# A long convolution and a spectral mix on one core: the last pair's loads move from GpSimd's queue to SyncE's, and two loops share their evictions anew

## The chip, the cores and the metric

The kernel runs on one core of a Trainium2 chip. The metric is device time in microseconds (us) of one execution, the median of three runs. PE is TensorE, DVE VectorE, ACT ScalarE, POOL GpSimd, SP SyncE. A DMA that POOL issues goes through a queue that the profile calls software_dynamic (q0); one that SP issues goes through hardware_dynamic (q1).

## The reference

x is 8 x 5696 x 128, h is 5696 x 128, all float32. First x is convolved with h along the sequence, each of the 128 channels by itself; then 64 Fourier modes of the result are mixed by complex 128 x 128 matrices and added to it, and a rectified product with a 128 x 128 matrix is added to that:

```python
def _attn_ref(x, h):
    L = 2 * S
    Yf = np.fft.rfft(x, n=L, axis=1) * np.fft.rfft(h, n=L, axis=0)[None, :, :]
    return np.fft.irfft(Yf, n=L, axis=1)[:, :S, :]

def _moe_ref(x, w_r, w_i, w_ch):
    X = np.fft.rfft(x, axis=1)
    Xr, Xi = np.real(X[:, :64]), np.imag(X[:, :64])
    Y = np.zeros_like(X)
    Y[:, :64] = (einsum(Xr, w_r) - einsum(Xi, w_i)) + 1j * (einsum(Xr, w_i) + einsum(Xi, w_r))
    u = x + np.fft.irfft(Y, n=S, axis=1)
    return u + np.maximum(u @ w_ch, 0.0)
```

## The kernel before, in words

The transforms are matrix products with constants, in float16. The sequence of 5696 is split as 89 x 64. The eight batches are worked in four pairs (`g_` from 0 to 3).

**First transform.** Per pair, 32 tiles (`a_tile`, `j` from 0 to 31) of four matmuls of 180 columns each turn the pair's x (tile Xin) into As; each tile goes to PSUM in two banks and one engine, DVE or ACT, casts it into SBUF (L313 and L317). With `eng` "both" each engine casts half of it. For pair 0 all 32 stand in a loop ahead of the passes, with six `filter_tick`s (the transform of h) between them; without an engine named, `evac` hands the tiles out in turn, ACT first. For the other pairs, tiles 0 to 5 stand in the last ticks of the pass before, and tiles 6 to 31 in a loop at the border of two passes: ACT the even ones, DVE the odd ones, tile 31 both.

**Passes.** A pass over a pair has 23 ticks (NT) of four frequencies, and three more to drain. In tick t PE makes the second transform (`second`, As by M), DVE multiplies by the filter (`products`, writes U), and for tick t - 2 PE multiplies U by Wc and ACT casts the result into one of 6 to 10 buffers Zs and Zt; SP then stores that buffer, 256 KB, to a scratch in DRAM (zscr). For tick t - 3 PE gathers the 64 modes with G. A buffer is cast into again only when its store has landed: in the last pair ten buffers serve the first ten stores, and from then on eight of them go round, so that store 18 takes the buffer of store 10, 21 that of 13.

**Loads of the last pass.** While pair 3 is worked, the last stage's inputs are loaded: W (the mode matrices, four parts of 1 MB), S4a, S4b and IBs (constants of the way back), and the first chunks of zscr, ZT0 to ZT3, each in two parts (1024 and 416 KB). `early` says in which tick which of them is issued. All of them stand on POOL, and `pace` makes POOL wait for the DVE product of that tick. ZT2 and ZT3 also wait for the first 15 stores of the pair to have landed (SLACK). `load_id`, a load of 32 KB, is issued by SP in tick 14 and waits (`ZY`) for the stores of buffers 8 and 9. Behind the pass come WI and ZT4, on POOL.

**Last stage.** PE makes the mode mix (XT by W), transposes it, and then works 16 chunks of zscr (`u_z`, `u_tile`; four a pair, five buffers ZT0 to ZT4) into u, and `o_tile` multiplies by WI; ACT makes R, DVE adds, SP stores 256 or 512 KB to the output. `load_zt(i + 5)` is issued on SP as soon as chunk i has been read.

**Order and waits.** The kernel writes every engine's instructions in the order of the program. A `Recorder` works out which of them must wait for which, by tokens: an instruction waits for the last writer of what it reads, and for the readers and the writer of what it overwrites. A wait stands on the engine that issues, so a DMA that waits holds up everything behind it on SP or POOL. Each DMA takes a semaphore of a ring, and waits until the one that had it before has landed (ring "t", "p", "q" and so on; "z" has 10 for the stores).

Of the kernel before, what the change touches and what calls it, by code (L numbers as in the profile page):

```python
# [4 lines left out]
P = 128  # L5
# [118 lines left out]
def bass_long_conv_fft__then__afno_spectral_mix_kernel(nc, x, h, moe_w_r, moe_w_i, moe_w_ch, out):  # L124
    B, S, D = x.shape
    M = moe_w_r.shape[0]
# [6 lines left out]
    NP = B // 2  # L133
    KT = 4
    NT = (NK + KT - 1) // KT
# [15 lines left out]
    c, s = np.cos(th), np.sin(th)  # L151
# [6 lines left out]
    s4 = np.stack([back[:, None, None] * np.cos(ang), -back[:, None, None] * np.sin(ang)], axis=0)  # L158
    RB, PB = 2 * NK - P, 32
    rows = s4.transpose(1, 0, 2, 3).reshape(2 * NK, S)  # L160
    SH = (J // 2 + 1) * NQ
# [11 lines left out]
    ib = modes.copy()  # L173
    ib[:, 0] *= 0.5
    ib = ib.T.reshape(P, NQ, J).transpose(0, 2, 1)
# [11 lines left out]
    def const(name, a):  # L187
        return nc.inline_tensor(np.ascontiguousarray(a.astype(np.float16)), name=name)
# [4 lines left out]
    c_s4 = const("cS4", s4t)  # L193
    c_ib = const("cIB", ib.reshape(P, -1)[:, 0:SH])
    c_sg = nc.inline_tensor(np.ascontiguousarray(sg.astype(np.float32)), name="cSG")
    c_g = const("cG", g)
    wd = nc.dram_tensor("wscr", [P, 2 * M * D], F16, kind="Internal")
# [8 lines left out]
    def at(name, cols, dt, off):  # L206
        return nc.alloc_sbuf_tensor_at(name, [P, cols], dt, offset=off)
# [23 lines left out]
    NZL = NZS[-1]  # L231
# [25 lines left out]
    NC = 5  # L257
    ZP = ZB * 2 * D
# [5 lines left out]
    zt = [[at(f"ZT{i}{'ab'[p_]}", ZP, F16, zt_off[i][p_]) for p_ in range(2)] for i in range(NC)]  # L264
    ib_sb = at("IBs", S, F16, a_m)
    s4_sb = [at("S4a", S, F16, a_m + 2 * S), at("S4b", S, F16, a_as)]
# [13 lines left out]
    w_sb = at("W", 2 * M * D, F16, a_x)  # L280
# [4 lines left out]
    def ap(t, row, p0, n, off, dims):  # L285
        return bass.AP(t, p0 * row + off, [[row, n]] + [list(d) for d in dims])
# [5 lines left out]
    def pv(bank, off, dims, p0=0, n=P):  # L292
        return bass.AP(ps, p0 * 4096 + bank * 512 + off, [[4096, n]] + [list(d) for d in dims])

    R = Recorder(nc)
    for name, n in (("c", 16), ("x", 26), ("z", 10), ("w", 16), ("t", 10), ("s", 8), ("o", 12), ("p", 16), ("q", 10)):
        R.ring(name, n)

    def bank(i):
        return ("bank", i)  # L300
# [18 lines left out]
    def dma(eng, dst, src, ring, reads=(), writes=(), after=()):  # L319
        R.add(eng, lambda h_: h_.dma_start(dst, src), reads, writes, ring=ring, after=after)  # L320

    def mm(o, l, r, st, sp, reads, writes):
        R.add("tensor", lambda h_: h_.matmul(o, l, r, start=st, stop=sp), reads, writes)  # L323
# [3 lines left out]
    def once(key, toks):  # L327
        if key in first:
            return []
        first[key] = 1  # L330
        return list(toks)
# [3 lines left out]
    def turns(name, items):  # L335
        i = ring2.get(name, 0)
        ring2[name] = i + 1
        return items[i % len(items)]
# [41 lines left out]
    WD = [p_[3] for p_ in wp]  # L380
# [25 lines left out]
    XIN = [("xin", i) for i in range(2 * XC)]  # L406
# [33 lines left out]
    for j in range(16):  # L440
        t = turns("h", [0, 2, 4])
# [5 lines left out]
        for i in range(4 if j < 15 else 26):  # L447
# [4 lines left out]
             eng="vector" if j in (3, 7) else "scalar")  # L452
        if j % 2:
            i = j // 2 % 2 * XC + j // 4
# [4 lines left out]
    AST = [("as", j) for j in range(33)]  # L459

    def a_tile(j, slots, eng=None):
        t = turns("s", slots) if len(slots) > 1 else slots[0]
        for i in range(4):
            d = 4 * j + i
            mm(pv(t + i // 2, (i % 2) * 2 * NK, [[1, 2 * NK]]),
               ap(x_sb, XW, 0, P, d, [[XS, 2 * J]]), f1_sb[:, :], True, True,
               XIN + XZ + [("f1",)], [bank(t + i // 2)])
        if eng == "both":
            for i, e in enumerate(("vector", "scalar")):
                evac(bass.AP(a_sb, 4 * j + 2 * i, [[AW, P], [D, 2 * NK], [1, 2]]), pv(t + i, 0, [[1, 2 * NK], [2 * NK, 2]]),  # L470
                     [bank(t + i)], [("as", j + i)], 1.0 / 64, eng=e, after=once(("hp", j), HP))
            return
        evac(bass.AP(a_sb, 4 * j, [[AW, P], [D, 2 * NK], [2, 2], [1, 2]]),
             pv(t, 0, [[1, 2 * NK], [512, 2], [2 * NK, 2]]),
             [bank(t), bank(t + 1)], [("as", j)], 1.0 / 64, eng=eng, after=once(("hp", j), HP))


    def xtok(n):
        return [("xt", n, p_) for p_ in range(2)]
# [30 lines left out]

    def load_w(i):
        w = 2 * M * D // 4
        dma("gpsimd", w_sb[:, i * w:(i + 1) * w], bass.AP(wd, i * w, [[2 * M * D, P], [1, w]]),
            "p", WD, [("w", i)] + (XIN if i == 0 else []), after=pace)

    H_ALL = [("h", t, 0) for t in range(NT)] + [("h", t, 1, p0) for t in range(NT) for p0 in (0, J)]
    U_ALL = [("u", i) for i in range(NU)] + [("xs", i) for i in range(NXS)] + \
# [1 line left out]
    M_ALL = [("m", i) for i in range(MP)]  # L519
# [3 lines left out]
    ZX = [("zs", i, b) for i in range(NZ, NZL) for b in range(2)]  # L523
    zt_old = [(H_ALL, H_ALL), (AST, AST), (AST, AST), (H_ALL, H_ALL), (M_ALL[3:6], G_ALL)]

    def load_zt(i, eng="sync", more=()):
        g_, c_ = divmod(i, J // ZB)
        for part, (p0, r0, n) in enumerate(((0, 0, P), (PB, P, RB))):
            old = list(once(("zt", i % NC, part), zt_old[i % NC][part])) + list(more) + pace
            dma(eng, bass.AP(zt[i % NC][part], p0 * ZP, [[ZP, n], [1, ZP]]),  # L530
                bass.AP(zs, (g_ * 2 * NK + r0) * J * 256 + c_ * ZB * 256, [[J * 256, n], [1, ZP]]),
                "q" if eng == "gpsimd" else "t", [("zd", g_, s_) for s_ in range(NT)], [("zt", i % NC, part)], after=old)

    def clear_zt(i):
        z32 = zt[i][1][0:PB, :].bitcast(U32)
        R.add("gpsimd", lambda e: e.memset(z32, 0), (), [("zt0", i)], after=list(zt_old[i][1]) + pace)

    def load_ib():
        dma("gpsimd", ib_sb[:, 0:SH], c_ib.ap(), "p", (), [("ib", 0)], after=M_ALL[0:2] + pace)

    def reflect(eng, t, n, col, key, after):
        MN = S - SH
# [6 lines left out]

    def load_s4(part):  # L550
        n = PB + RB if part else P
        dma("gpsimd", s4_sb[part][0:n, 0:SH], bass.AP(c_s4, part * SH, [[2 * SH, n], [1, SH]]), "p", (),
            [("s4", part, 0)], after=pace + (AST if part else M_ALL[1:4]))

    V, A = "vector", "scalar"
    border = {NT - 1: [(0, 0, V)], NT: [(1, 2, V), (2, 0, V)], NT + 1: [(3, 2, A), (4, 0, V)], NT + 2: [(5, 2, V)]}
    early = {3: lambda: load_w(2), 5: lambda: load_w(3), 8: lambda: load_s4(1),
             10: lambda: clear_zt(0),
             11: lambda: load_zt(0, "gpsimd"),
             14: lambda: (load_id(), clear_zt(1)),  # L560
             15: lambda: load_zt(1, "gpsimd"),
             16: lambda: load_s4(0),
             18: lambda: load_ib(),
             NT - 2: lambda: (load_zt(2, "gpsimd", SLACK), load_zt(3, "gpsimd"), clear_zt(2), clear_zt(3))}
    pace = []
    SLACK = [("zd", NP - 1, s_) for s_ in range(NT - NZL)]

    def load_id():
        dma("sync", id_sb[:, :], bass.AP(c_w, 2 * P, [[3 * P, P], [1, P]]), "c", (), [("id",)], after=ZY)
# [144 lines left out]
    for i in range(NXH):  # L714
        x_load(1, i, x_h[i], xtok(i), [t_ for r_ in XR for t_ in r_])
    FOUR = [0, 2, 4, 6]
    for j in range(32):
        a_tile(j, FOUR)
        if j >= 11 and j % 3 == 2 and (j - 11) // 3 < LH:
            h_ = turns("s", FOUR)  # L720
            filter_tick((j - 11) // 3, [h_, h_ + 1])
    keep(16, turns("s", FOUR))
    for g_ in range(NP):
        if g_ == NP - 1:
            load_w(0)
            load_w(1)
        for t in range(NT + LM):
            tick(g_, t)
            if g_ == 0 and t < 2:
                keep(8, 4)  # L730
            assert g_ + 1 < NP or not wp
            if g_ == NP - 1 and t in early:
                pace[:] = [("u", min(t, NT - 1) % NU)]
                early[t]()
        evac(bass.AP(xt, 2 * g_ * XTW + M, [[B * XTW, P], [XTW, 2], [1, P]]), pv(MB, 0, [[P, 2], [1, P]]),
             [bank(MB)], [("xt", g_)], 1.0 / 64, eng="scalar", after=[("ag", k) for k in range(NS + 2 * XN, NK)])
        evac(bass.AP(xt, 2 * g_ * XTW, [[B * XTW, P], [XTW, 2], [1, M]]), pv(MB, M, [[P, 2], [1, M]]),
             [bank(MB)], [("xtn", g_)], -1.0 / 64, eng="vector" if g_ + 1 == NP else "scalar", after=[("ag", k) for k in range(NS + 2 * XN, NK)])
        if g_ + 1 < NP:
            for j in range(6, 32):  # L740
                a_tile(j, [(4, 6, 0, 2)[(j - 7) % 4] if j > 6 else 0], "both" if j == 31 else V if j % 2 else A)
                if j == 31:
                    keep(8, 6)
                if wp and j % 2 == 1:
                    dst, src_, ring, tok = wp.pop(0)
                    dma("gpsimd", dst, src_, ring, (), [tok], after=[("as", j)])
# [2 lines left out]
    pace[:] = []  # L749
    load_wi()  # L750
    for i in range(4, NC):
        load_zt(i, "gpsimd")
        clear_zt(i)

    LSLOT = [0, 2, 4, 6]
# [62 lines left out]
    for hb in range(2):  # L818
        evac(bass.AP(y_sb, hb * 32 * B, [[2 * M * B, P], [B, 32], [M * B, 2], [1, B]]),
             pv(6 + hb, 0, [[2 * B, 32], [B, 2], [1, B]]), [bank(6 + hb)], [("y", hb)], eng="vector" if hb else "scalar",  # L820
             after=ZY)
# [66 lines left out]
    for g_ in range(NP):  # L888
        last = g_ == NP - 1
        order = [(c_, b) for b in range(2) for c_ in range(NCH)] if last else [(c_, b) for c_ in range(NCH) for b in range(2)]  # L890
        for n, (c_, b) in enumerate(order):
            i = NCH * g_ + c_
# [46 lines left out]
```

## Time and profile before

| what | us |
|---|---|
| median of three runs | 384.41 |
| lowest, highest | 383.37, 386.99 |
| profiled execution | 387.21 |
| its span, first to last instruction of the program | 385.1 |
| PE busy in the span | 362.4 (94%) |
| ACT busy | 314.3 (82%) |
| DVE busy | 296.6 (77%) |
| POOL busy | 85.2 (22%) |
| passes of pairs 0 to 3 begin (first second transform) | 43.5, 106.8, 162.2, 217.7 |
| last cast of the last pass ends | 262.6 |
| last instruction of the chain | 381 |

The table's times count from the first instruction of the program in the profiled execution. PE's busy time is a model of pipelined matmuls, so 94% is not 94% of what PE can do. A PE clock of 1.00 is the full one. DMA traffic is told per queue: packets, MB moved, and the time that its packets took as a share of 16 engines' time; shares of two queues that overlap can add up to more than 100%.

### The profile page before, as it was taken

To read this page: it belongs to the slowest core of one execution; us is meant where nothing else is said; L and a number is where in the kernel's file an instruction comes from. 1 tells how busy PE (TensorE), PEld (TensorE's weight loads), DVE (VectorE), ACT (ScalarE), POOL (GpSimd) and SP (SyncE) were. 2 spreads that over 40 slices of the span, in tenths; PEclk is the share of its full clock that TensorE was granted. 3 is DMA by queue.
4 is the path that set the end of the run, shared out by engine and by line. 5 is a ranking of instruction groups with operands and counts; after the bars stand their busy time and mean duration, and the time that the engine had idled before them with its cause. 6 is when DMAs were issued, how large, how long until landed. Compare 5 with 4: busy or idle time off the path is not lost.

```text
span 385.1 us, 12438 instructions
## 1 busy us (share of the span) xinstructions
PE 362.4 (94%) x5346; PEld 280.7 (73%) x5346; DVE 296.6 (77%) x336; ACT 314.3 (82%) x491; POOL 85.2 (22%) x134
## 2 busy tenths in 40 slices
PE   7989899999989999999999899978999999999994
PEld 7878766667856667756667666648789989888873
DVE  3649899988988998989999988761537767766665
ACT  8469699898989997899998899965447777688884
POOL 8812012100733311823203213307200000000000
PEclk9999999999999999999999999995799999999999
DMA  7999969977999995999995799999999999999877
GB/s 148 206 298 354 243 139 249 250 220 222 97 126 215 249 268 151 132 134 232 243 274 114 95 325 357 327 367 292 392 391 362 367 416 403 419 405 383 325 293 316
DMA packets 87137, 103.94 MB, mean 270 GB/s; under 512 B 22819, under 2 KB 72611, under 8 KB 83527
## 3 DMA queue, kind: packets, MB, share of 16 engines
q1 hardware_dynamic: 62603, 67.76, 50.7%
q0 software_dynamic: 24480, 35.40, 44.2%
q8 instruction: 42, 0.69, 0.7%
q14 instruction: 12, 0.10, 0.1%
HBM read 70.61 MB, written 51.12 MB: 316 GB/s over the span
## 4 chain that ended last, share of the span: by engine, by line
PE 76%; DMA 8%; DVE 6%; ACT 4%; POOL 3%; issue 2%; DVEq 0%; ACTq 0%; POOLq 0%
PE ps L323 76%; DMA Xr<-in_x_dram 4%; DMA zscr<-Zs 3%; DVE As L317 2%; DVE U L630 2%; POOL Xr L320 2%; ACT As L313 2%; ACT R L871 1%; POOL Hin L320 1%; DVE Xin L365 1%; DVE Hs L315 1%; ACT Zt L311 1%; ACT Zs L311 0%; DMA Hs<-Hs 0%; ACT Xs L311 0%
## 5 line engine op out<-in xcount | busy, mean ns | idle before, releaser
L323 PE MATMUL ps<-U,Wc 128*128 128x512 f16 (+1 forms) x368 | 94.4, 377 | 4.2 <-ACT Zs L311 3.7
L638 DVE TENSOR_TENSOR U<-Xs,Hs 128x2048 f16<-128x2048 f16 (+1 forms) x73 | 86.9, 1192 | 13.8 <-ACT Xs L311 13.1
L311 ACT CAST Xs<-ps 128x1024 f16<-128x1024 f32 (+1 forms) x77 | 75.1, 979 | 12.6 <-PE ps L323 7.6
L311 ACT CAST Zs<-ps 128x512 f16<-128x512 f32 (+1 forms) x132 | 69.3, 592 | 5.5 <-DMA zscr<-Zs 3.8
L872 DVE TENSOR_TENSOR O<-ps,R 128x512 f32<-128x512 f32 x81 | 52.3, 685 | 20.1 <-ACT R L871 11.2
L317 DVE TENSOR_SCALAR As<-ps 128x720 f16<-128x720 f32 x70 | 57.7, 886 | 5.2 <-PE ps L323 4.6
L871 ACT ACTIVATE R<-ps 128x512 f32<-128x512 f32 (+1 forms) x92 | 50.5, 591 | 8.5 <-PE ps L323 8.4
L323 PE MATMUL ps<-F,Xin 128*128 128x180 f16 x512 | 53.7, 249 | 3.9 <-DVE Xin L365 2.6
L323 PE MATMUL ps<-As,M 64*128 64x128 f16 x1440 | 50.3, 217 | 3.5 <-DVE U L630 2.9
L323 PEld LDWEIGHTS ps<-F,Xin 128*128 128x128 f16 x512 | 44.4, 155 | 12.6 <-DVE As L317 2.8
L323 PEld LDWEIGHTS ps<-U,Wc 128*128 128x128 f16 x368 | 28.6, 97 | 33.3 <-ACT Zs L311 7.6
L313 ACT ACTIVATE As<-ps 128x720 f16<-128x720 f32 (+1 forms) x61 | 45.7, 769 | 7.9 <-PE ps L323 6.5
L323 PE MATMUL ps<-WI,UT 128*128 128x256 f16 x360 | 51.1, 278 | 0.5 <-ACT UT L311 0.4
L311 ACT CAST UT<-ps 128x712 f16<-128x712 f32 x46 | 34.5, 752 | 19.2 <-PE ps L323 18.0
L323 PEld LDWEIGHTS ps<-As,M 64*128 64x128 f16 x1440 | 40.6, 94 | 9.7 <-DVE U L630 3.6
L323 PEld LDWEIGHTS ps<-WI,UT 128*128 128x128 f16 x360 | 39.1, 152 | 3.4 <-issue 1.8
L323 PE MATMUL ps<-IBs,C 128*128 128x356 f16 x128 | 40.3, 324 | 0.1
L320 POOL DMA_DIRECT2D Xt<-in_x_dram x40 | 21.1, 533 | 80.8 <-PE ps L323 80.3
L323 PEld LDWEIGHTS ps<-G,Zs 128*128 128x128 f16 x512 | 26.3, 97 | 14.3 <-ACT Zs L311 1.6
L638 DVE TENSOR_TENSOR U<-ps,Hs 128x2048 f16<-128x2048 f32 x15 | 34.3, 2284 | 0.0
L323 PE MATMUL ps<-G,Zs 128*128 128x128 f16 (+2 forms) x512 | 32.4, 193 | 0.0
L311 ACT CAST Zt<-ps 128x512 f16<-128x512 f32 x52 | 28.5, 624 | 0.3 <-PE ps L323 0.3
(88 smaller groups left out, 504.7 us busy)
## 6 DMA issues: line engine op xcount, KB each, us to landing
out_dram<-O SPq DMA_DIRECT2D x39, 512.0 KB, 7.6
zscr<-Zs SPq DMA_DIRECT2D x62, 256.0 KB, 7.0
zscr<-Zt SPq DMA_DIRECT2D x26, 256.0 KB, 6.8
Xt<-in_x_dram POOLq DMA_DIRECT2D x20, 320.0 KB, 7.1
W<-wscr POOLq DMA_DIRECT2D x4, 1024.0 KB, 8.2
M<-cM POOLq DMA_DIRECT2D x5, 720.0 KB, 16.9
ZT0a<-zscr SPq DMA_DIRECT2D x3, 1024.0 KB, 8.8
Hs<-Hs SPq DMA_DIRECT2D x44, 64.0 KB, 6.3
```

Source lines behind the costliest of these rows:

```text
L311: R.add(e, lambda h_: h_.copy(dst, src), reads, writes, after=after)
L313: R.add(e, lambda h_: h_.activation(dst, src, COPY, scale=scale), reads, writes, after=after)
L315: R.add(e, lambda h_: h_.tensor_copy(dst, src), reads, writes, after=after)
L317: R.add(e, lambda h_: h_.tensor_scalar_mul(dst, src, scale), reads, writes, after=after)
L320: R.add(eng, lambda h_: h_.dma_start(dst, src), reads, writes, ring=ring, after=after)
L323: R.add("tensor", lambda h_: h_.matmul(o, l, r, start=st, stop=sp), reads, writes)
L365: R.add("vector", lambda e: e.tensor_copy(bass.AP(x_sb, i * XN * XS, [[XW, NQ], [XS, XN], [1, D]]), src), list(toks) + XZ, [("xin", i)])
L630: R.add("vector", lambda e, b=b, s_=s_: e.tensor_tensor(bass.AP(u_s[i], b * 512, [[2048, P], [1024, 2], [1, n * D]]), s_, hv, MULT), [tok, ...
L638: R.add("vector", lambda e: e.tensor_tensor(uv, src, hv, MULT), bk + [("h", t, 0), ("h", t, 1, 0), ("h", t, 1, J)], [("u", i)])
L871: R.add("scalar", lambda e: e.activation(rv, src_r, RELU), bk, [("r", i % NR)], after=once(("r", i % NR), G_ALL + XTT + [("y", 0), ("y", 1 ...
L872: R.add("vector", lambda e: e.tensor_tensor(ov, src_u, rv, ADD), bk + [("r", i % NR)], [key + (h_,)], after=once(key, old))
```

## The change

It has two parts. In the last pass, the loads of W, S4a, S4b, IBs and ZT0 to ZT4 are issued by SP, each behind the store of a given tick, without `pace` and without SLACK; the ticks of some are set anew, and ring "t" gets 20 semaphores. POOL keeps the clearing of ZT's padding, with its `pace`.

| tick | before (POOL) | after (SP) |
|---|---|---|
| before tick 0 | W0, W1 | W0, W1 |
| 3, 5 | W2, W3 | W2, W3 |
| 8 | S4b | S4b |
| 10 | | ZT0 |
| 11 | ZT0 | |
| 12 | | S4a |
| 14 | Id (on SP) | Id, IBs |
| 15 | ZT1 | |
| 16 | S4a | ZT1 |
| 18 | IBs | |
| 19 | | ZT3 |
| 21 | ZT2, ZT3 behind 15 stores | ZT2 |
| behind the pass | ZT4 | ZT4 |

The other part is the first transform. In the loop for pair 0 each tile's engine is written out (DVE starts, 16 tiles on ACT and 15 on DVE), and tile 31 goes half to each. At a border, tiles 6 to 30 go by a pattern of nine, five of them ACT's, so that ACT has 14 and DVE 11 of them, where it was 13 and 12.

```diff
-        dma("gpsimd", w_sb[:, i * w:(i + 1) * w], bass.AP(wd, i * w, [[2 * M * D, P], [1, w]]),
-            "p", WD, [("w", i)] + (XIN if i == 0 else []), after=pace)
+        dma("sync", w_sb[:, i * w:(i + 1) * w], bass.AP(wd, i * w, [[2 * M * D, P], [1, w]]),
+            "p", WD, [("w", i)] + (XIN if i == 0 else []))
...
-    def load_zt(i, eng="sync", more=()):
+    def load_zt(i):
...
-            old = list(once(("zt", i % NC, part), zt_old[i % NC][part])) + list(more) + pace
-            dma(eng, bass.AP(zt[i % NC][part], p0 * ZP, [[ZP, n], [1, ZP]]),
+            old = list(once(("zt", i % NC, part), zt_old[i % NC][part]))
+            dma("sync", bass.AP(zt[i % NC][part], p0 * ZP, [[ZP, n], [1, ZP]]),
...
-        dma("gpsimd", ib_sb[:, 0:SH], c_ib.ap(), "p", (), [("ib", 0)], after=M_ALL[0:2] + pace)
+        dma("sync", ib_sb[:, 0:SH], c_ib.ap(), "p", (), [("ib", 0)], after=M_ALL[0:2])
...
-             10: lambda: clear_zt(0),
-             11: lambda: load_zt(0, "gpsimd"),
-             14: lambda: (load_id(), clear_zt(1)),
-             15: lambda: load_zt(1, "gpsimd"),
-             16: lambda: load_s4(0),
-             18: lambda: load_ib(),
-             NT - 2: lambda: (load_zt(2, "gpsimd", SLACK), load_zt(3, "gpsimd"), clear_zt(2), clear_zt(3))}
+             9: lambda: clear_zt(0),
+             10: lambda: load_zt(0),
+             12: lambda: load_s4(0),
+             14: lambda: (load_id(), load_ib(), clear_zt(1)),
+             16: lambda: load_zt(1),
+             19: lambda: (load_zt(3), clear_zt(3)),
+             NT - 2: lambda: (load_zt(2), clear_zt(2))}
...
+    SHARE = [V if c_ == "V" else A for c_ in "VAVAAVAVAVAVAVAVAVAAVVAVAVAVAVA"]
     for j in range(32):
-        a_tile(j, FOUR)
+        a_tile(j, FOUR, "both" if j == 31 else SHARE[j])
...
-                a_tile(j, [(4, 6, 0, 2)[(j - 7) % 4] if j > 6 else 0], "both" if j == 31 else V if j % 2 else A)
+                a_tile(j, [(4, 6, 0, 2)[(j - 7) % 4] if j > 6 else 0], "both" if j == 31 else (A, V)[(j - 6) % 9 % 2])
...
-        load_zt(i, "gpsimd")
+        load_zt(i)
```

More of the change, by code (lines that the diff above doesn't have):

```diff
@@ L295, in bass_long_conv_fft__then__afno_spectral_mix_kernel @@
     R = Recorder(nc)
-    for name, n in (("c", 16), ("x", 26), ("z", 10), ("w", 16), ("t", 10), ("s", 8), ("o", 12), ("p", 16), ("q", 10)):
+    for name, n in (("c", 16), ("x", 26), ("z", 10), ("w", 16), ("t", 20), ("s", 8), ("o", 12), ("p", 16), ("q", 10)):
         R.ring(name, n)
@@ L524, in bass_long_conv_fft__then__afno_spectral_mix_kernel @@
     zt_old = [(H_ALL, H_ALL), (AST, AST), (AST, AST), (H_ALL, H_ALL), (M_ALL[3:6], G_ALL)]
-    def load_zt(i, eng="sync", more=()):
+    def load_zt(i):
         g_, c_ = divmod(i, J // ZB)
         for part, (p0, r0, n) in enumerate(((0, 0, P), (PB, P, RB))):
-            old = list(once(("zt", i % NC, part), zt_old[i % NC][part])) + list(more) + pace
-            dma(eng, bass.AP(zt[i % NC][part], p0 * ZP, [[ZP, n], [1, ZP]]),
+            old = list(once(("zt", i % NC, part), zt_old[i % NC][part]))
+            dma("sync", bass.AP(zt[i % NC][part], p0 * ZP, [[ZP, n], [1, ZP]]),
                 bass.AP(zs, (g_ * 2 * NK + r0) * J * 256 + c_ * ZB * 256, [[J * 256, n], [1, ZP]]),
-                "q" if eng == "gpsimd" else "t", [("zd", g_, s_) for s_ in range(NT)], [("zt", i % NC, part)], after=old)
+                "t", [("zd", g_, s_) for s_ in range(NT)], [("zt", i % NC, part)], after=old)
     def clear_zt(i):
@@ L551, in load_s4 @@
         n = PB + RB if part else P
-        dma("gpsimd", s4_sb[part][0:n, 0:SH], bass.AP(c_s4, part * SH, [[2 * SH, n], [1, SH]]), "p", (),
-            [("s4", part, 0)], after=pace + (AST if part else M_ALL[1:4]))
+        dma("sync", s4_sb[part][0:n, 0:SH], bass.AP(c_s4, part * SH, [[2 * SH, n], [1, SH]]), "p", (),
+            [("s4", part, 0)], after=AST if part else M_ALL[1:4])
     V, A = "vector", "scalar"
@@ L557, in bass_long_conv_fft__then__afno_spectral_mix_kernel @@
     early = {3: lambda: load_w(2), 5: lambda: load_w(3), 8: lambda: load_s4(1),
-             10: lambda: clear_zt(0),
-             11: lambda: load_zt(0, "gpsimd"),
-             14: lambda: (load_id(), clear_zt(1)),
-             15: lambda: load_zt(1, "gpsimd"),
-             16: lambda: load_s4(0),
-             18: lambda: load_ib(),
-             NT - 2: lambda: (load_zt(2, "gpsimd", SLACK), load_zt(3, "gpsimd"), clear_zt(2), clear_zt(3))}
+             9: lambda: clear_zt(0),
[5 more added lines that the diff above has]
+             NT - 2: lambda: (load_zt(2), clear_zt(2))}
     pace = []
-    SLACK = [("zd", NP - 1, s_) for s_ in range(NT - NZL)]
     def load_id():
```

## The prediction

> **What bounds the kernel now.** I read the page first, then the chain of waits, then the waits, the timeline and the DMA issues of the stretch in which the page shows a fall. On the page PE is busy 94% of the span, so another engine's time counts only where PE waits. The one row that is not flat is the granted clock: about 5 and 7 tenths in slices 28 and 29, where everything else is 9.
>
> ```profile
> PEclk9999999999999999999999999995799999999999
> ```
>
> Busy times by stretch around it (columns: PE, PEld, DVE, ACT, POOL, granted clock, DMA share, GB/s):
>
> ```profile
> 257.90:260.40 2.50, 0.02 (x1) 0.00 (x0) 0.00 (x0) 0.00 (x0) 0.00 (x0) 1.00 1.04 321
> 260.40:274.10 13.70, 12.27 (x213) 10.83 (x214) 4.53 (x6) 7.01 (x10) 10.05 (x11) 0.50 0.98 329
> 274.10:280.00 5.90, 5.90 (x112) 5.23 (x110) 2.07 (x3) 2.48 (x4) 0.00 (x0) 1.00 1.02 388
> ```
>
> At 257.9 all engines stop for over 2.5 us while DMA is full; then PE runs for 13.7 us at half the clock. The waits of that stretch (us, times, longest) say who ended the stop, and the chain of waits (start, us) which DMA it was:
>
> ```profile
> ACT Zs L311 <- DMA zscr<-Zs: 3.8, 1, 3.8
> PE ps L323 <- ACT Zs L311: 3.7, 1, 3.7
> ```
>
> ```profile
> 247.65 0.20 ACT Zs L311
> 247.86 13.02 DMA zscr<-Zs
> ```
>
> A store of 256 KB, issued at 247.86, landed 13.02 us later. I call store n the one of tick n's products, which the loop makes in tick n + 2. Counted from the pass's first cast this is store 13 of the last pair; ACT's cast for store 21 takes the same buffer, and stood. The DMA rows tell why it was slow: in 248 to 254 both kinds of queue had work waiting, and moved
>
> ```profile
> q0 software_dynamic: 280, 1.80, 78.6%
> q1 hardware_dynamic: 967, 0.44, 25.7%
> ```
>
> (packets, MB). q0 is POOL's loads, q1 SP's stores: the stores got 0.44 MB in 6 us, 73 GB/s, where the pass makes one store of 0.262 MB per tick of about 1.7 us, 154 GB/s. The loads in flight were ZT1 (1.475 MB in two parts) and S4a (0.752), issued between 246.67 and 247.73, and IBs at 251.27. After the stop, the same pair of matmuls shows the clock (start, length):
>
> ```profile
> 263.04 0.28 PE L323 MATMUL ps<-S4a,ZT0a 128*128 128x89 f16 x1
> ...
> 263.19 0.28 PE L323 MATMUL ps<-S4a,ZT0a 128*128 128x89 f16 x1
> ...
> 274.27 0.20 PE L323 MATMUL ps<-S4a,ZT0a 128*128 128x89 f16 x1
> ...
> 274.36 0.20 PE L323 MATMUL ps<-S4a,ZT0a 128*128 128x89 f16 x1
> ```
>
> A pair starts every 0.15 us in the slow stretch, every 0.09 us after it.
>
> **Part 1: the loads go from POOL to SP.** Seventeen DMA issues move (4 W, 2 S4, IBs, 10 of ZT0 to ZT4). POOL loses them at 0.53 to 0.56 us each, and nothing waited for POOL's issuing, so that is worth nothing. SP gains them at 0.33 us (its own ZT0a issue at 274.76) to some 0.5, 6 to 9 us over the pass; SP waits 108.9 us for ACT's Zs over the run, which covers it. What matters is order: loads and stores now stand in one queue, q1, served in order of issue, as the last stage (q1 alone) shows by landing its DMAs in the order of issue. A store is then late by what was issued ahead of it, and not for as long as a load is in flight beside it.
>
> So I add up what is ahead of each store. The casts end as in the profile (for store 13 at 245.5), W0 and W1 are issued at 218.7, the first bytes move at about 220. Up to store 13 the queue holds W 4.194, S4b 0.493, ZT0 1.475, S4a 0.752, IBs 0.752 and fourteen stores, 3.67: 11.3 MB. The rate: 368 GB/s in 232 to 240, 376 in 248 to 254, 311 in 240 to 248 where SP stood, 321 in the stop. At 350 the queue is through that store at 252.4, landed by 253; ACT wants it at 257.18. Stores 10, 11, 12 and 14, whose buffers are used again too, come out 4 to 6 us early. Store 13 is too late only under 310 GB/s.
>
> The new waits on SP: load_id in tick 14 still waits for store 9 to land (SP stood 3.4 us for it before). That store is now behind ZT0, and lands at about 245.7 by the same sum, against 247.47 before; IBs and stores 13 and 14 stand behind it, which the sum has in it. ZT0 and ZT3 wait for the DVE product of their tick, one tick at most, with the next store behind them. ZT2 no longer waits for the first 15 stores to land. None takes the margin of 4 us.
>
> Worth: ACT's wait, **3.8 us**. Then the clock. From the last Zs cast (262.62) to the first ZT1 matmul (274.76) it takes 12.14 us at half clock. At full clock PE's part shrinks to 0.09/0.15 of it, 7.3 us, somewhat less for the small matmuls; then PE waits for the others where it did not before: for XT (ACT 0.38, DVE 0.29), for Y on DVE (0.69), for C (0.60) and for the first UT behind the IBs reflection (1.56) on DVE, some 0.35 us each by these rows. I take 8.3 us, so **3.8 us** more. Bounds: 6.1 if all halves, 0 if the clock falls all the same. Behind 274.76 the stage is PE's (no wait of PE over 0.6 us in it), and what is won before is won at the end.
>
> [...]
>
> Does the last stage have its data? Up to ZT2, now issued behind store 19, the queue holds 17.3 MB: at 350 GB/s it lands at 270, and is wanted at 271.2 (274.76 - 7.6 + 4.1, the time a chunk takes from ZT1 to ZT2 at 278.9). ZT3 is ahead of it, ZT4 wanted at 279 and landed by 276. Loads move faster than stores, so I expect 3 us to spare. Later the issues are 7.6 us earlier in the same queue; their peak time to landing was 13.2 us (out at 338.45), and I get about 14, where seven O buffers at 2.65 us a pair allow some 16.
>
> **Part 2: the first-transform tiles.** A tile costs DVE 0.83 and ACT 0.72 us back to back (9.52 us for 11.5, 1.44 for 2). In a border DVE has 11.5 from tile 7, ACT 13.5; one tile moves over, so DVE gets 9.6 us of work and ACT 10.5 from 95.6. Both ended at about 106.65; the ACT sum ends near 106.3. Bounds: 0.8 us better (DVE's tile gone, ACT in its gaps), 0.5 worse (ACT bound, no gaps). I take 0.1 to 0.2 each, 0.4 for three. In the first loop ACT has 16.5 tiles and 5 filter casts, DVE 15.5 and one; the last tile was DVE's alone, ending at 43.39 with ACT done at 42.69. Halved, both end near 43.0: **0.4 us** (-0.4 to 1.0). The 128x360 half takes 0.55 us in the borders.
>
> **Sum**, against the profiled execution of 387.21 us (span 385.1 and 2.1 around it): 387.2 - 3.8 - 3.8 - 0.4 - 0.4 = 378.8. That execution is 2.8 us above the median of 384.41. If all runs have the whole stall, the median goes to 376.0; if the 2.8 us are stall that the others lack, to 378.8. I take **377.0**.
>
> **Rivals.**
> A, slower: ZT2 comes late. It is issued in tick 21 behind ZT3 and twenty stores. If q1 moves 310 GB/s instead of 350, 17.3 MB take until 276.3, 5.1 us after 271.2. That stop is longer than the one of 257.9, so the clock halves again, and 13.7 us at 0.50 lose 13.7 x 0.43 = 5.8: 10.9 lost against 8.4 won, 387; at 300 GB/s 389. Under about 330 GB/s the gain is gone bit by bit. For it: 308 GB/s was the mean of 218 to 248. Against: q0 was empty in parts of that.
> B, the last stage becomes DMA's. From 303 to 338 q1 moved 394 GB/s and was full. At 30 GB/s less the same sum gives 19 us from issue to landing, 3 over the 16 that the buffers allow, and those 3 us and what they push go on DVE and so on PE: 380 to 383. Against: no O waits for a DMA now, and 2.95 MB of loads are moved ahead.
> C, the clock falls in spite of it, since PE is half idle behind the last tick in any case: only 3.8 + 0.8, so 380. Against: at the other borders gaps of 0.85 us leave it at 1.00.
> D, nothing: the bytes and the 16 DMA engines are the same, and stores are as late in one queue as in two: 384. The rows above speak against it, with 1.80 MB to 0.44 between two queues that both had work. [...]
>
> **How the numbers follow.** Forecast 0.64 (374 to 380), A 0.12 (384 to 391), B 0.10, C 0.07, D 0.07. Within 1% of 384.41 is 380.6 to 388.3, about what a measurement tells from no change. Faster: 0.64 and half of B and C, 0.73. Slower: half of A, 0.06. Same: the rest, 0.21. For 8 in 10 the range goes from 373 (both ends of the tiles' gain) to 384.5: it takes in B, C and D, and leaves out A's worse part and the ends.
>
> **What would show it.** Right: no ACT Zs wait for a store in the last pass; granted clock 1.00 there; ZT1's first matmul near 267; stores 10 to 14 landing 4 to 10 us after issue; the tile stage ending near 43.1 and the borders 0.1 to 0.4 us shorter. Wrong: a PE wait for ZT2, a second stretch at 0.50, DVE's O waiting for out_dram, or SP standing long behind load_id. It would also be wrong if the runs without a profile hold less of the stall than the profiled one.

## The result, and the profile after

The changed kernel takes 381.94 us (median of 18 runs, 380.29 to 383.07), the kernel before 384.25 (18 runs, 381.85 to 386.99): a ratio of 0.9944, 95% interval 0.9921 to 0.9968. It is faster by 2.3 us, 0.6%, where 7.4 us were forecast; 381.94 lies inside the 1% (380.6 to 388.3) that the prediction took for no change. A ratio, here and below, is not the quotient of the two medians shown, and it leaves out executions more than 1.5% above the fastest of their kernel (four of twelve in the run with the new ticks on POOL, at most two elsewhere). The two profiled executions lie further apart, 387.21 and 381.70 us, with spans of 385.1 and 379.9.

The page's row of the granted clock:

```profile
PEclk9999999999999999999999999998899999999999
```

It still dips in slices 28 and 29, only less. Busy times by stretch (PE, PEld, DVE, ACT, POOL, clock, DMA share, GB/s):

```profile
257.90:259.40 1.50, 1.23 (x26) 1.00 (x22) 0.42 (x2) 1.07 (x3) 1.41 (x2) 1.00 1.12 430
259.40:262.27 2.87, 2.87 (x89) 2.86 (x89) 1.65 (x1) 2.55 (x2) 0.92 (x1) 1.00 1.04 377
262.27:269.10 6.83, 6.60 (x99) 5.41 (x97) 2.79 (x4) 2.05 (x4) 0.00 (x0) 0.50 1.03 363
269.10:275.00 5.90, 5.90 (x111) 5.23 (x110) 2.12 (x3) 2.35 (x4) 0.00 (x0) 1.00 1.00 388
```

The stop is gone: PE works 1.23 of 1.50 us where before nothing ran. But at 262.27 the clock halves all the same, after 2.87 us in which PE was busy without a break, and for 6.83 us against 13.65 before. Both lengths are multiples of 3.41 us, two and four times; a piece of that length, counted from the fall, is called a window below. The mode mix (PE and PEld of the matmuls that read W alone, then clock, DMA share, GB/s) lies in the window ahead of the fall and in the first slow one, and not in the second:

```profile
258.86:262.27 3.41, 2.54 (x73) 2.40 (x73) 1.00 1.04 387
262.27:265.68 3.41, 1.81 (x59) 1.70 (x56) 0.50 1.11 382
265.68:269.10 3.42, 0.00 (x0) 0.00 (x0) 0.50 0.95 344
```

ACT's casts of the last three ticks now follow each other, which is what the stop's end looks like when the buffer is free (start, us, count):

```profile
255.44 2.65 ACT L311 CAST Zs<-ps 128x512 f16<-128x512 f32 x6
258.49 0.38 ACT L313 ACTIVATE XT<-ps 128x256 f16<-128x256 f32 x1 [0.40 <-PE ps L323]
```

Store 13, which took 13.02 us before, and the one queue in 248 to 254:

```profile
zscr<-Zs SPq DMA_DIRECT2D x1, 256.0 KB, 6.1
```

```profile
q1 hardware_dynamic: 1562, 2.09, 104.1%
```

Where the 5.2 us of span went, by marks in the two traces (us):

| from, to | before | after | gain |
|---|---|---|---|
| start to the last pass's first second transform | 217.65 | 217.01 | 0.64 |
| that to ZT0's first matmul (pass and stop) | 45.24 | 41.28 | 3.96 |
| ZT0's to ZT1's first matmul (mix, transposes) | 11.87 | 11.43 | 0.44 |
| ZT1's to the end | 110.32 | 110.14 | 0.18 |

The third row is the one that the forecast put at 3.8. That the profiles differ by 5.2 us and the medians by 2.3 is a second question.

### The profile page after: what moved, and what is told of

Its sections match the earlier page's. It is cut to its first block, busy times and chain, and to the rows that moved or that the text cites. A ratio compares the mean times of both kernels' runs of the same rounds, so it can differ in the third digit from the quotient of the medians.

```text
span 379.9 us, 12434 instructions
## 1 busy us (share of the span) xinstructions
PE 359.7 (95%) x5346; PEld 278.9 (73%) x5346; DVE 294.9 (78%) x333; ACT 314.4 (83%) x495; POOL 75.1 (20%) x117
## 4 chain that ended last, share of the span: by engine, by line
PE 66%; ACT 13%; DVE 7%; DMA 6%; issue 4%; POOL 3%; DVEq 0%; ACTq 0%; POOLq 0%
PE ps L323 65%; ACT As L313 7%; DMA Xr<-in_x_dram 4%; DVE As L317 2%; ACT Zs L311 2%; DMA zscr<-Zs 2%; DVE U L629 2%; ACT Zt L311 2%; POOL Xr L320 2%; ACT Xs L311 1%; DVE Xin L365 1%; ACT R L871 1%; POOL Hin L320 1%; DVE U L637 1%; DVE Hs L315 1%
## 5 line engine op out<-in xcount | busy, mean ns | idle before, releaser
L872 DVE TENSOR_TENSOR O<-ps,R 128x512 f32<-128x512 f32 x81 | 52.3, 684 | 20.1 <-ACT R L871 11.2
L317 DVE TENSOR_SCALAR As<-ps 128x720 f16<-128x720 f32 (+1 forms) x67 | 55.6, 880 | 5.7 <-PE ps L323 4.0
L323 PE MATMUL ps<-F,Xin 128*128 128x180 f16 x512 | 52.4, 250 | 3.7 <-DVE Xin L365 2.2
```

The source lines that it names most:

```text
L317: R.add(e, lambda h_: h_.tensor_scalar_mul(dst, src, scale), reads, writes, after=after)
L872: R.add("vector", lambda e: e.tensor_tensor(ov, src_u, rv, ADD), bk + [("r", i % NR)], [key + (h_,)], after=once(key, old))
```

## The experiments

Each result is given as time and as ratio to the kernel before on the same chip, with the interval. "Upper group" stands for the executions of a kernel with a long stretch at half clock; each run lists its mean granted clock, and a share of 0.987 or less marks most of them, but not only them: two profiled executions without a stop (the loads alone, 0.985, and the new ticks on POOL, 0.984) have one more 3.41 us at 0.50 at 28 us, where the first loop is 1.0 us longer for it. The kernel before ran 110 times beside the experiments: 48 had 0.987 or less, with a mean of 385.4 us, the other 62 a median of 382.6. The execution whose profile the prediction read (387.21, clock 0.980) belongs to the first kind, and to its end: only five of the 110 had 0.981 or less. None of the 43 with 0.983 to 0.987 was profiled; that they have a shorter stop is inferred from their times.

**The loads alone.** The changed kernel, with

```diff
-        a_tile(j, FOUR, "both" if j == 31 else SHARE[j])
+        a_tile(j, FOUR)
...
-                a_tile(j, [(4, 6, 0, 2)[(j - 7) % 4] if j > 6 else 0], "both" if j == 31 else (A, V)[(j - 6) % 9 % 2])
+                a_tile(j, [(4, 6, 0, 2)[(j - 7) % 4] if j > 6 else 0], "both" if j == 31 else V if j % 2 else A)
```

> The changed kernel with the tiles shared out as before: the loads' part alone. Theory M (the clock falls because the mode mix's 16-column matmuls use too little of the array in a window of about 3.4 us, stop or no stop; the loads' part is worth the stop alone): in the profile no ACT wait for a store, ZT0's first matmul to ZT1's about 11.4 us with a stretch at 0.50 of one to three windows, span about 380.5; in time 1.5 to 2.0 us below the kernel before, less than the profile's 4, if the stop is shorter in other executions than in the profiled one. Theory S (PE standing lowers the clock, and the changed kernel's fall was chance): ZT0 to ZT1 about 8.5 us at 1.00, time 5 us or more below.

382.73 us (381.74 to 383.23), ratio 0.9967 (0.9935 to 0.9998). No execution reached 384, where 11 of 29 of the kernel before did. The median lies at that of the kernel before's other executions (382.59): where there is no stop, the loads' part gives nothing. No wait of ACT for a store; ZT0 to ZT1 11.56 us, 6.83 of them at 0.50. As M has it.

**The tiles alone.** The kernel before with `SHARE` and the pattern of nine.

> The kernel before with the new sharing of the tiles: that part alone. Both theories: the last pass begins 0.6 us earlier than before's 217.65 (0.36 of it in the first loop, 0.3 at a border, some lost again), stop of 2 to 4 us and 0.50 for three or four windows as before; time 0.4 to 0.8 us below the kernel before.

383.09 us (380.86 to 386.46), ratio 1.0011 (0.9975 to 1.0048): unclear in time, since 5 of 12 lie at 384 or more. In the profile the part does what it should: last Xin copy to last As cast 16.44 before, 16.09 here, in the first loop; 19.75 to 19.49, 16.34 to 16.09 and 16.33 to 16.08 at the borders. But its profiled execution, with POOL's loads as before, held a surprise for both theories:

```profile
255.00:258.55 3.55, 3.41 (x40) 2.00 (x39) 1.39 (x2) 3.35 (x8) 2.33 (x5) 1.00 1.04 380
258.55:262.73 4.18, 4.01 (x117) 3.85 (x115) 3.38 (x2) 3.56 (x3) 4.18 (x4) 1.00 1.10 397
262.73:269.56 6.83, 6.60 (x94) 5.25 (x91) 2.78 (x4) 2.00 (x3) 3.39 (x5) 0.50 1.05 399
```

There is no stop, and the 6.83 us at half clock are those of the changed kernel. So the stop is not in every execution of the old loads.

**The stop filled.** The kernel before, with spare matmuls where PE stood:

```diff
             zb = [turns("z", ZBANK) for b in range(2)]
+            if g_ == NP - 1 and s_ == NT - 1:
+                keep(48, 2)
```

> The kernel before with 48 spare matmuls of 180 columns (3.6 us of PE) put ahead of the last tick's transform of the last pair, where PE stood: nothing that it computes changes. M: the clock stays 1.00 through the stop, falls all the same one or two windows into the mode mix, at about 264, and is back after two or three windows (7 to 10 us); ZT0 to ZT1 11.3 to 11.9. S: 1.00 throughout, ZT0 to ZT1 about 8.5.

One execution, 385.30 us. The spare matmuls run from 257.21 to 261.09, the mix lies in 262.2 to 268:

```profile
257.50:262.20 4.70, 4.61 (x64) 4.38 (x61) 0.00 (x0) 0.97 (x3) 4.70 (x5) 1.00 1.11 375
262.20:266.00 3.80, 3.60 (x104) 3.48 (x102) 1.14 (x2) 3.26 (x3) 3.80 (x6) 1.00 1.01 403
266.00:272.83 6.83, 6.60 (x104) 5.40 (x101) 2.79 (x4) 2.13 (x4) 1.00 (x1) 0.50 0.99 371
```

The clock holds through them and falls 3.8 us behind ZT0's first matmul, as in the changed kernel (4.0). S is out: PE need not stand for the clock to fall here. Nor need it be half idle behind the last tick, as rival C had it: it was busy 4.61 of 4.70 us there.

**Spare matmuls in the mix.** The changed kernel, with every second, fourth and eighth mode followed by one (k = 2, 4, 8):

```diff
+            if m % k == k - 1:
+                mm(pv(4, 0, [[1, 2 * NK]]), f1_sb[:, 0:P], f1_sb[:, :], True, True, [("f1",)], [bank(4)])
```

> The changed kernel with one spare matmul of 180 columns behind every second mode of the mix, 32 in all, 2.4 us of PE. M: the array is used enough, the clock stays 1.00; ZT0 to ZT1 is 11.4 - 1.5 + 2.4 = 12.3 and the time 0 to 1 us above the changed kernel's. S or any theory in which the tail of the pass lowers the clock: still 0.50 for two windows, ZT0 to ZT1 13.8, time 2.4 us above.

> The changed kernel with one spare matmul of 180 columns behind every fourth mode, 16 in all, 1.2 us of PE. M, if that is use enough: clock 1.00, ZT0 to ZT1 11.4 - 1.7 + 1.2 = 10.9, 0.5 us below the changed kernel. M, if it is not: 0.50 for one or two windows, 12.0 to 12.6, 0.5 to 1.2 us above.

> The changed kernel with one spare matmul of 180 columns behind every eighth mode, 8 in all, 0.6 us of PE. M: between the two; if 8 still suffice, clock 1.00 and ZT0 to ZT1 10.3, 1 us below the changed kernel; if not, 0.50 for one or two windows, 11.5 to 12, 0 to 0.6 us above it.

ZT0's to ZT1's first matmul as a stretch, for 32, 16 and 8 spare ones:

```profile
259.17:271.31 12.14, 11.41 (x244) 10.54 (x242) 4.84 (x6) 5.40 (x6) 1.93 (x2) 1.00 1.03 362
```

```profile
257.51:268.36 10.85, 10.13 (x229) 9.26 (x226) 4.84 (x6) 5.40 (x6) 1.92 (x2) 1.00 1.04 361
```

```profile
257.64:267.96 10.32, 9.61 (x221) 8.73 (x219) 4.84 (x6) 5.40 (x6) 1.92 (x2) 1.00 1.04 378
```

All at 1.00 in these profiles. Less their 2.4, 1.2 and 0.6 us (0.075 each, 180 columns: the first row has 24 more than the last and is 1.82 us longer) that is 9.7 us each time. So the full clock makes the stretch 9.7 us and not 8.3, and the half clock costs the changed kernel 11.4 - 9.7 = 1.7 us. Times: 382.81 (ratio 0.9976, 0.9945 to 1.0007), 381.02 (0.9942, 0.9913 to 0.9972) and 380.83 us (0.9918, 0.9887 to 0.9949). The last is the lowest median of all runs. That eight hold the clock is shown by one profile; three of that kernel's ten executions have a clock share of 0.992 or 0.993 where the others have 0.996 to 0.999, which is what one more 3.41 us at 0.50 takes, and where those lie is not known.

**Id's load later.** Store 13 had been issued behind SP's wait at `load_id`, so I took that wait for the cause of the stop. The kernel before, with

```diff
-             14: lambda: (load_id(), clear_zt(1)),
+             14: lambda: clear_zt(1),
...
-             18: lambda: load_ib(),
+             18: lambda: (load_id(), load_ib()),
```

> The kernel before with the 32 KB load of Id in tick 18 instead of 14, nothing else. Theory H (the stop comes when SP stands at that load, which waits for store 9: store 13 is then issued behind ZT1 and S4a and starved; where store 9 lands early SP does not stand and there is no stop): store 13 issued at about 245.5 in every execution, no ACT wait for a store, and no execution in the upper group of the kernel before (384 to 387, clock share 0.986 or less, 11 of 29); median 0.5 to 1 us below. Rival Q (it is enough that loads are in flight in the other queue): the upper group stays, a third of the executions, median unchanged.

383.26 us (382.01 to 388.60), ratio 1.0000 (0.9968 to 1.0032), 5 of 12 at 384 or more. H falls: the profiled execution (388.60) has a stop with SP not standing at Id. Its wait and its store 13, issued at 246.9:

```profile
ACT Zs L311 <- DMA zscr<-Zs: 2.8, 2, 2.4
```

```profile
zscr<-Zs SPq DMA_DIRECT2D x1, 256.0 KB, 14.4
```

**The ticks without the queue.** The kernel before, with the changed kernel's table of ticks, all loads but Id on POOL.

> The kernel before with all loads on POOL's queue, but in the ticks of the changed kernel and without ZT2's and ZT3's wait: the ticks without the queue, tiles shared out as before. If the queue is what matters: stores 9 to 14 land 8 to 14 us after issue with ZT0, S4a and IBs beside them, SP stands at Id as often or more, and half of the executions or more lie at 384 to 387, with a stop of 2 to 6 us in the profile. If the ticks are what matters: no upper group, 382 to 383 as with the loads' part alone.

384.95 us (381.72 to 389.50), ratio 1.0034 (1.0000 to 1.0069); 9 of 12 at 384 or more. So it is the queue that helps; the new ticks by themselves hurt, if anything. The profiled execution (384.07) had no stop; the rest is from times and clocks. POOL's queue and SP's also differ in kind (software_dynamic and hardware_dynamic): no run put the loads on a second queue of SP's kind, so whether it is the one queue that helps, or leaving POOL's, is open.

**The changed kernel again.**

> The changed kernel itself on the same chip, to set beside the others: no execution above 383.5, median 0.8 below the loads' part alone by the tiles (0.35 in the first loop, 0.25 at each border); in the profile no ACT wait for a store, one to three windows at 0.50 in the mix, ZT0 to ZT1 11.2 to 11.9.

382.30 us (381.08 to 384.31), ratio 0.9974 (0.9948 to 1.0000), and 1 of 12 at 384 or more, against 16 of 35. ZT0 to ZT1 11.86 us, 6.83 at 0.50. Its 0.8 us below the loads' part came as 0.4 between two chips' medians, and is not settled by times.

**Why only some executions stop.** In those with a stop the first loads were late: W0 issued 1.0 us behind the last pass's first matmul in the kernel before and 0.6 in the run with Id later (0.15 in the tiles' run, but 0.7 in the new ticks' run, which had no stop either), and W1 landed 2.8 us behind W0 (3.5 in the run with Id later), against 2.5 in the others. Two runs on the kernel before delay them and bring them forward:

```diff
-            load_w(0)
-            load_w(1)
+            pass
...
-    early = {3: lambda: load_w(2), 5: lambda: load_w(3), 8: lambda: load_s4(1),
+    early = {0: lambda: (load_w(0), load_w(1)), 3: lambda: load_w(2), 5: lambda: load_w(3), 8: lambda: load_s4(1),
```

> The kernel before with W0 and W1 issued behind tick 0's product, some 2 us later, nothing else. In the profiles with a stop W1 landed 2.8 and 3.5 us behind W0, in those without 2.5, and W0 was issued 1 us later against the pass. Theory L (lateness of the first loads is what the stores cannot make up): the upper group (384 to 389) takes most executions, median 385 or more. Theory D (the DMAs of some executions are slower as such, lateness adds little): the upper group stays at a third to a half, median within 1 us of the kernel before.

386.26 us (385.89 to 388.42), ratio 1.0068 (1.0030 to 1.0105): all ten executions in the upper group. The profiled one has the stop, and then the same 13.65 us at half clock:

```profile
ACT Zs L311 <- DMA zscr<-Zs: 2.9, 1, 2.9
```

```profile
260.88:274.53 13.65, 13.31 (x223) 11.71 (x224) 4.46 (x6) 6.70 (x10) 10.04 (x11) 0.50 1.04 359
```

```diff
-                if wp and j % 2 == 1:
+                if wp and (j % 2 == 1 or g_ == 2):
```

> The kernel before with the last six conversions of the mode matrices issued behind six tiles in a row of the last border instead of every second one: W0 can start 0.5 to 1.5 us earlier. L: the upper group shrinks to a tenth or less, median 0.5 us below. D: a third as before, median unchanged.

382.94 us (380.97 to 384.92), ratio 0.9972 (0.9938 to 1.0005); 4 of 12 at 384 or more, none at 385, where the kernel before had 13 of 33 at 385 or more. Less than L expected, but in its direction. So lateness is enough: some 2 us of it put every execution into the upper group. That lateness is also what parts the executions of the kernel before is not shown; D can still be part of it, since W1 itself came slowly in those with a stop.

**Both remedies.** The 16 spare matmuls and the earlier conversions in the changed kernel.

> The changed kernel with 16 spare matmuls in the mix and the conversions of the mode matrices earlier as well. M: clock 1.00, ZT0 to ZT1 10.9, 1.0 to 1.5 us below the changed kernel; the earlier W changes nothing there, since no store is late in one queue.

381.34 us (380.37 to 382.57), ratio 0.9925 (0.9896 to 0.9954). In one queue the earlier W changes nothing that these times show.

**The delay in one queue.** Is the changed kernel safe, or are its first loads only early? W0 and W1 behind store 0:

```diff
-            load_w(0)
-            load_w(1)
+            pass
...
-    early = {3: lambda: load_w(2), 5: lambda: load_w(3), 8: lambda: load_s4(1),
+    early = {2: lambda: (load_w(0), load_w(1)), 3: lambda: load_w(2), 5: lambda: load_w(3), 8: lambda: load_s4(1),
```

> The changed kernel with W0 and W1 issued behind store 0, some 5 us later than now and 1 us later than in the run that delayed them on POOL. If one queue is what makes the stores safe from late loads: no ACT wait for a store, no execution with a stop, a clock share of 0.985 to 0.992, median within 1 us of the changed kernel's 382. If lateness costs the same in one queue (its stores are then 2 MB further behind): a stop of 2 us or more, 385 to 388 in most executions, as with POOL.

382.04 us (380.69 to 383.19), ratio 0.9956 (0.9930 to 0.9981). W0 was issued at 222.2, 1 us later than in the run that stopped every time. Store 13 landed 6.4 us after issue here, 11.2 there; first this kernel, then that one:

```profile
zscr<-Zs SPq DMA_DIRECT2D x1, 256.0 KB, 6.4
```

```profile
zscr<-Zs SPq DMA_DIRECT2D x1, 256.0 KB, 11.2
```

No ACT wait for a store, no execution with a clock share under 0.988. In SP's one queue such a delay left the stores on time.

## Why the prediction was wrong

**Right: the stop, its cause and its end.** Stores starved beside loads of the other queue: store 13 took 13.02 us, and 6.1 in one queue, where what SP issued from 217.13 to 264.47 landed in order of issue, from 222.0 to 273.9, wherever the trace has the landing. The sum along the queue had store 13 landed by 253 (it landed at 252.8), store 9 at 245.7 (245.76), ZT2 at 270 (268.4), ZT4 by 276 (273.9; for both the first part, the second's landing is not in the trace). That the landings agree so closely is in part luck: W0 was issued 1.6 us earlier than the sum took (217.13 against 218.7), so by the same sum the queue moved about 335 GB/s, not 350. Removing the stop gave 3.96 us between the two profiles, 3.8 forecast. Rivals A, B and D did not come: no PE wait for ZT2, no O wait for a store; the peak time to landing of an output was 12.9 us. (Rival B's 394 GB/s is the rate of 300 to 320; in 303 to 338 all queues moved 411.)

**Wrong, the step "at full clock PE's part shrinks ... I take 8.3 us, so 3.8 us more".** It took the stop for the cause of the whole slow stretch. The measured gain is 0.44 us, near the bound of 0 that the text gave "if the clock falls all the same". Two things were wrong in it. First, the clock falls at the mode mix without any stop (6.83 us at 0.50 in the changed kernel). The mix's 128 matmuls have 16 columns and start about 30 ns apart, in lots of 32 or 64 with 89-column ones between the lots, and with 8, 16 or 32 spare wide ones among them the clock stayed at 1.00. What it is about the small ones is not shown: that they use too little of the array, as M has it, is the author's guess. Rival C had the fall at 0.07, and blamed the drain of the pass for it. The stop only made the slow stretch begin earlier and last four windows of 3.41 us and not two. In the traces of before and after the last slow window is the first in which PE is busy throughout and no 16-column matmul runs (3.41 of 3.41 us and 3.42 of 3.42; in the window ahead of it 3.19 and 3.18, with 64 and 59 of them): with the stop the windows ahead of it hold the end of the stop and then the mix, without it the mix alone. Second, the mix does not speed up with the clock. Before, at 0.50, and after, at 1.00, the first two lots of 32:

```profile
264.09 1.14 PE L323 MATMUL ps<-XT,W 128*128 128x16 f16 x32
265.62 1.14 PE L323 MATMUL ps<-XT,W 128*128 128x16 f16 x32
```

```profile
259.37 1.11 PE L323 MATMUL ps<-XT,W 128*128 128x16 f16 x32 [0.20 <-issue]
260.67 1.11 PE L323 MATMUL ps<-XT,W 128*128 128x16 f16 x32
```

Both take 1.1 us. The ratio 0.09/0.15 of the 89-column pairs was applied to 3.9 us of such matmuls ("somewhat less for the small matmuls" was not priced). Left unscaled, these 3.9 us add 0.4 x 3.9 = 1.6 to the 8.3, which makes 9.9; measured are 9.7. So of the 3.8 us forecast, 0.4 came, 1.7 went to the fall that stayed, and the rest, about 1.6, was never there.

**Wrong, the step from the profiled execution to the median.** The text held that either all runs have the whole stall (376.0) or that the 2.8 us between profile and median are stall that the others lack (378.8), and took 377.0. The second is nearer to what came: the changed kernel's profiled executions have no stop, and the first of them (381.70) lies at the median (381.94). Of the 4.9 us between 377.0 and 381.94, 1.8 come from taking 377.0 and not 378.8; the other 3.1 are mostly the clock's term (3.8 forecast, 0.44 measured). Of 110 executions 62 had a clock share over 0.987 and a median of 382.6, which is what the loads' part alone gives. For these the loads' part is worth nothing. The other 48 lie 2.7 us above that in the mean, times 48 in 110, so 1.2 us in the mean of all.

**The tiles: right in kind, a little better.** 0.35 us in the first loop (0.4 forecast) and 0.25 at each border (0.13): 1.1 in all. Of these 0.64 us had arrived by the last pass in the profiled execution; the first pass was 0.55 us longer there (51.66 us to its last cast against 51.11), and that length varies by more between runs (50.64 to 52.36 us). In time the part is not resolved.

Together 1.2 and 1.1 make 2.3 us, the measured difference; that it agrees so well is chance, since the share of executions with a clock of 0.987 or less goes from 38% to 55% between batches, and the changed kernel measured again was only 0.9 us below the kernel before (382.30 against 383.19).

## What to carry to other kernels

A stall that waits for a DMA may be there in one execution and not in the next (a wait of 3.8 us in one profile with the old loads, none in another): before a gain is forecast from one profile, look at the spread and the clock shares of the other runs, and ask which of them have the stall. Bulk loads that run beside small stores were better off here in the stores' queue, behind them, where each store's landing can be added up; a late start then cost nothing that the times show (a ratio of 0.9956 against 0.9944), where with two queues it cost 2 us (386.26 against 384.40). A fall of the clock is to be traced to the matmuls of the few us ahead of it and not only to the gap in sight; where they are small, a few wide spare ones can cost less than the fall (here 0.6 or 1.2 us against 1.7, while 32 of them, 2.4 us, cost more).

## What the runs showed of the hardware

Eight spare matmuls of 180 columns, 0.6 us in all, held the clock at 1.00 through the mix in the one profile taken of them, and with none there it fell in every profile taken (11 of 11, at 0.50 for 6.83 us in eight and 13.65 us in three, two or four times 3.41; their mean granted clock was 0.979 to 0.990, and 0.996 to 0.999 in the four with spare ones in the mix). Why eight are enough is not shown, and fewer were not tried.

PE's busy row did not tell of the fall: in the changed kernel 2.87 of 2.87 us were busy ahead of it, and 3.21 of the last 3.41 us. Nor was PE idle at 0.50: it was at work for 12.27 of 13.70 us before and for 6.60 of 6.83 after.

Two queues with work did not share evenly by bytes or by packets: in 248 to 254 of the kernel before, 1.80 MB in 280 packets went to the loads and 0.44 MB in 967 to the stores. By the same two rows (78.6% and 25.7%) the packets of a MB of loads took 44% of the 16 engines' 6 us, those of a MB of stores 58%: in that sense loads did move faster than stores. And with the first loads delayed by some 2 us all ten executions took 385.9 us or more; the profiled one had a wait of 2.9 us at the end of a pass of 40 us and 13.65 us at half clock behind it. What makes the first loads late in some executions only stays open: the conversions of W landed up to 0.9 us later against the pass in these (0.48 us behind its first matmul in the kernel before, 0.41 ahead of it in the tiles' run), and W1 came at 304 and 369 GB/s against about 420 (its 1.05 MB over the time from W0's landing to its own), but no run set that rate.
